# Decode attention with a long cache on one core: the second product moved to quarters of the PE array, output columns dealt, `wo` in smaller pieces

## The chip, the cores and the metric

One core of a Trainium2 chip runs the kernel. The metric is the device time in microseconds (us) of one execution, taken without a profile. All runs here are on one core; runs are called fast unless one is clearly off (one execution of 982 us among the runs of the kernel before and two of the six of e8 are such, and are left out of the ratios). TensorE is called PE below, VectorE DVE and ScalarE ACT, as in the profile. A product on PE has a stationary operand, the weights, which is loaded first (PEld in the profile), and a moving one, which is streamed through in columns; SBUF is the memory on the chip that holds the operands, PSUM the one that takes the sums. The granted clock is the share of its full clock that PE was allowed in a stretch. A landing is the moment at which a transfer's data have arrived.

## The reference

One token attends to a cache of 65,536 keys; beside it runs a small gated MLP, and a sigmoid gate mixes the two. Cut to what matters:

```python
# x (1,1,1024); 32 query heads in 4 groups of 8; K and V caches (1,4,65536,128), bfloat16
q = x @ wq                                    # 1024 x 4096
scores = q . k * 128**-0.5                    # 8 heads share one group's K and V
p = softmax(scores)                           # over 65536 keys
o = p . v                                     # the "second product"
a = o.reshape(4096) @ wo                      # 4096 x 1024
b = gated_mlp(x)  @ w_out                     # w_in 1024 x 3584, w_out 1792 x 1024
out = sigmoid(x . gate_w) * a + (1 - ...) * b # (1,1,1024), bfloat16
```

The caches are 128 MiB, all inputs 162 MB. Every byte is read once.

## The kernel before

K and V come in tiles of 128 chunks; a chunk is 128 keys, and a tile of 4 MiB is one DMA. K chunks are transposed on PE, copied to SBUF by DVE and ACT, and multiplied with the queries, which gives scores with the keys on the partitions. Five buffers (`NKV`) take all large loads in turn. The parts that the change touches:

```python
LAG = 4
WO_SPLIT = ((16,), (8, 4, 2, 1, 1))     # wo in two buffers: one piece of 16 chunks, then 8, 4, 2, 1, 1
...
    def v_units(g, j, vt):               # second product: V chunk stationary, scores moving
        ...
            for i in range(TG):          # one product for each chunk of 128 keys
                ...
                nc.tensor.matmul(o_ps[g][:, o0:o0 + wv], lhsT=vt[:, c, :],
                                 rhs=scT[g][:, lo:hi, :].rearrange("p c h -> p (c h)"),
                                 start=False, stop=(cg == NCG - 1), skip_group_check=True)
...
    def project(w, n, vec, c0, first=False, last=False):   # used for w_out and for wo
        for c in range(n):
            for j in range(NJ):                             # NJ = 8
                nc.tensor.matmul(
                    out_ps[:, j, :], lhsT=w[:, c, j * P:(j + 1) * P],
                    rhs=vec[:, c0 + c:c0 + c + 1].to_broadcast([P, W]),
                    start=(first and c == 0 and j == 0), stop=(last and c == n - 1),
                    skip_group_check=True)
...
    out_sb = const.tile([P, NJ], FP32, name="out_sb")
    nc.vector.tensor_copy(out=out_sb[:], in_=out_ps[:, :, 0])
    outT_ps = psm.tile([NJ, P], FP32, name="outT_ps", tag="m")
    nc.tensor.transpose(outT_ps[:], out_sb[:], ident_f[:])
    outT = const.tile([NJ, P], BF16, name="outT")
    nc.vector.tensor_copy(out=outT[:], in_=outT_ps[:])
    nc.sync.dma_start(out=out.rearrange("o t (j p) -> (o t j) p", p=P), in_=outT[:])
```

In the second product every chunk of V is loaded as weights, for only 8 useful columns of scores. The weights of `project` are 128 neighbouring columns.

## Time and profile before

| | before |
|---|---|
| time, median of 4 runs (of 3 when predicted: 393.51) | 393.16 us |
| span of the profiled execution | 390.8 us |
| PE busy | 78% |
| DMA share from 20 to 375 us | 1.00 to 1.01, about 429 GB/s |

These lines are from the page of the kernel before: busy time by engine, three lines of the 40 slices (each digit a tenth of the slice), and two DMA queues with packets, MB and their share of the time of 16 engines.

```profile
PE 306.5 (78%) x7080; PEld 296.8 (76%) x7080; DVE 152.3 (39%) x296; ACT 122.3 (31%) x139; POOL 1.0 (0%) x9
...
PE   0774379998888879778888888697979697996946
...
DMA  8999999999999999999999999999999999999972
GB/s 329 426 444 429 441 426 430 434 429 428 429 428 426 431 423 431 429 434 429 424 426 436 424 429 431 423 434 423 428 427 434 436 434 429 434 421 428 433 330 114
...
q1 hardware_dynamic: 6208, 162.01, 96.8%
q8 instruction: 55, 0.90, 0.8%
```

The DMA line is the one to read: nine tenths or more in every slice between the first and the last two. From the sixth slice on PE has mostly digits of 6 to 9 and waits for data. The second to last slice shows something else: 330 GB/s. Three windows of the same trace, with the stretch, its length, busy time of each engine, granted clock, DMA share and GB/s:

```profile
370.00:375.00 5.00, 2.06 (x67) 1.94 (x63) 0.00 (x0) 0.00 (x0) 0.00 (x0) 0.90 1.00 424
375.00:378.00 3.00, 0.25 (x5) 0.26 (x6) 0.00 (x0) 0.00 (x0) 0.00 (x0) 0.50 0.83 341
378.00:387.00 9.00, 8.60 (x237) 8.50 (x235) 0.00 (x0) 0.00 (x0) 0.00 (x0) 0.84 0.49 198
```

From 378 to 387 us half of the DMA engines have run out of work. The trace also holds every increment that an engine makes to a transfer's semaphore when its part has landed, sixteen for each large transfer. For the last piece of `wo` they fall into two groups of eight:

```
kernel before, last piece of wo, us of each engine's landing
377.14 377.19 377.48 377.52 377.88 378.10 378.30 379.78
385.90 386.22 387.18 387.25 387.29 387.30 387.34 387.43
```

The kernel ends soon after the slower eight. The timeline of its end, with start, duration, engine and line, operation, and in brackets what ended the idle time before it:

```profile
368.31 3.63 PEld L402 LDWEIGHTS <-wout_t 128*128 128x128 bf16 x112
368.42 3.64 PE L402 MATMUL out_ps<-uT,wout_t 128*128 128x64 bf16 x112
...
377.75 7.13 PE L402 MATMUL out_ps<-oa,wo_t 128*128 128x64 bf16 x182 [5.69 <-DMA wo_t<-in_A_wo_dram]
385.29 2.61 PE L402 MATMUL out_ps<-oa,wo_t 128*128 128x64 bf16 x74 [0.41 <-issue]
387.93 0.17 DVE L433 COPY out_sb<-out_ps 128x8 f32<-128x8 f32 x1 [18.79 <-PE out_ps L402]
388.15 0.08 PEld L435 LDWEIGHTS outT_ps<-ident_f,out_sb 128*8 128x8 f32 x1 [0.38 <-DVE out_sb L433]
388.15 0.27 PE L435 MATMUL outT_ps<-ident_f,out_sb 128*8 128x128 f32 x1 [0.26 <-DVE out_sb L433]
388.46 0.28 DVE L437 CAST outT<-outT_ps 8x128 bf16<-8x128 f32 x1 [0.37 <-PE outT_ps L435]
388.77 0.36 SPq L438 DMA_DIRECT2D out_dram<-outT  x1
```

The projection of w_out takes 3.6 us for 112 products, which start 31 ns apart, at a granted clock of 1.00. The first 58 products of `wo` start 53 ns apart, for the granted clock is 0.50 there; the others again 31 ns. PE is done 0.5 us after the last piece has landed (387.43). Then 0.84 us of copy, transpose and copy, and 2.0 us from the issue of the result's DMA to the end.

### The profile page before, as it was taken

The page shows a single profiled execution, that of the slowest core. Times are in us where ns is not written, and L with a number is a line of the kernel's source. Part 1 is how long each engine was busy: PE and PEld are TensorE (multiplying, and loading weights), DVE is VectorE, ACT ScalarE, POOL GpSimd, SP SyncE. Part 2 cuts the span into 40 slices and gives each one's busy share as a digit, 9 for nine tenths or more (in the row PEclk, how much of TensorE's full clock was granted, in tenths as well). Part 3 has the DMA queues.
Part 4 walks back from the last instruction along what each step waited for, and adds up shares of the span by engine and source line. Part 5 has one row for each costly group of instructions (what it writes and reads, how often), then busy time and mean ns, then how long its engine had stood idle before and what let it go on. Part 6 is the DMA issues. An engine that isn't in the chain of part 4 may idle for free.

```text
span 390.8 us, 14957 instructions
## 1 busy us (share of the span) xinstructions
PE 306.5 (78%) x7080; PEld 296.8 (76%) x7080; DVE 152.3 (39%) x296; ACT 122.3 (31%) x139; POOL 1.0 (0%) x9
## 2 busy tenths in 40 slices
PE   0774379998888879778888888697979697996946
PEld 0764379887888779778888878696979697896846
DVE  2011036665684335336534543275434345300100
ACT  1010025554574323324543333244524242300000
POOL 1000000000000000000000000000000000000000
PEclk9999999999999989999999999899989899899869
DMA  8999999999999999999999999999999999999972
GB/s 329 426 444 429 441 426 430 434 429 428 429 428 426 431 423 431 429 434 429 424 426 436 424 429 431 423 434 423 428 427 434 436 434 429 434 421 428 433 330 114
DMA packets 6305, 162.96 MB, mean 417 GB/s; under 512 B 740, under 2 KB 740, under 8 KB 1124
## 3 DMA queue, kind: packets, MB, share of 16 engines
q1 hardware_dynamic: 6208, 162.01, 96.8%
q8 instruction: 55, 0.90, 0.8%
q14 instruction: 6, 0.05, 0.0%
q10 hardware_dynamic: 36, 0.00, 0.0%
HBM read 162.01 MB, written 0.00 MB: 415 GB/s over the span
## 4 chain that ended last, share of the span: by engine, by line
PE 55%; DMA 32%; issue 7%; ACT 3%; DVE 1%; SPq 0%; ACTq 0%
PE tps L322 27%; DMA kn<-in_A_k_cache_dram 24%; PE spt L301 13%; PE o_ps L355 11%; DMA wo_t<-in_A_wo_dram 9%; PE out_ps L402 2%; PE o_ps L344 1%; ACT ktt L325 1%; ACT scT L288 1%; ACT scT L307 1%; SPq L84 0%; PE nb_ps L279 0%; DVE mxr L264 0%; DVE mxr L309 0%; PE mxT L271 0%
## 5 line engine op out<-in xcount | busy, mean ns | idle before, releaser
L322 PE MATMUL tps<-ident_b,kn 128*128 128x128 bf16 x2048 | 164.0, 224 | 25.6 <-DMA kn<-in_A_k_cache_dram 12.8
L327 DVE COPY ktt<-tps 128x1024 bf16<-128x1024 bf16 x171 | 116.6, 689 | 123.4 <-PE tps L322 122.9
L322 PEld LDWEIGHTS <-kn 128*128 128x128 bf16 x2048 | 124.0, 100 | 28.8 <-issue 15.3
L325 ACT COPY ktt<-tps 128x1024 bf16<-128x1024 bf16 x85 | 85.9, 1012 | 156.0 <-PE tps L322 156.0
L355 PE MATMUL o_ps<-scT,vt 128*128 128x64 bf16 (+1 forms) x2048 | 104.4, 200 | 14.4 <-issue 11.5
L301 PE MATMUL spt<-qT,ktt 128*128 128x64 bf16 (+7 forms) x2048 | 102.9, 193 | 8.9 <-issue 7.0
L355 PEld LDWEIGHTS <-vt 128*128 128x128 bf16 x2048 | 88.5, 101 | 17.0 <-issue 12.9
L301 PEld LDWEIGHTS <-ktt 128*128 128x128 bf16 x2048 | 85.6, 99 | 10.6 <-issue 8.2
L307 ACT CAST scT<-spt 128x512 bf16<-128x512 f32 x32 | 18.9, 589 | 24.8 <-PE spt L301 15.9
L344 PE MATMUL o_ps<-scT,ones_b 128*128 128x256 bf16 x64 | 18.1, 283 | 2.1 <-issue 1.4
L288 ACT ACTIVATE scT<-scT 128x1024 bf16<-128x1024 bf16 x16 | 16.4, 1056 | 6.2 <-DVE scT L284 6.2
L309 DVE TENSOR_TENSOR mxr<-scT,mxr 128x512 bf16<-128x512 bf16 x24 | 10.2, 425 | 15.8 <-ACT scT L307 14.3
L185 PE MATMUL z_ps<-xT,win_t 128*128 128x18 bf16 x224 | 13.7, 210 | 1.3 <-DMA win_t<-in_B_w_in_dram 0.8
L185 PEld LDWEIGHTS <-win_t 128*128 128x128 bf16 x224 | 13.7, 158 | 1.3 <-DMA win_t<-in_B_w_in_dram 0.9
L402 PE MATMUL out_ps<-oa,wo_t 128*128 128x64 bf16 x256 | 9.7, 204 | 6.1 <-DMA wo_t<-in_A_wo_dram 5.7
L402 PEld LDWEIGHTS <-wo_t 128*128 128x128 bf16 x256 | 9.4, 105 | 6.4 <-DMA wo_t<-in_A_wo_dram 5.8
L237 PE MATMUL q_ps<-xT,wq_t 128*128 128x1 bf16 x256 | 7.1, 165 | 7.5 <-DMA wq_t<-in_A_wq_dram 7.5
L361 DVE TENSOR_TENSOR lm<-sel_q,o_ps 128x32 f32<-128x32 f32 x4 | 0.7, 182 | 31.3 <-PE o_ps L355 31.3
L237 PEld LDWEIGHTS <-wq_t 128*128 128x128 bf16 x256 | 7.0, 104 | 7.6 <-DMA wq_t<-in_A_wq_dram 7.6
L284 DVE TENSOR_TENSOR scT<-scT,negm 128x1024 bf16<-128x1024 bf16 x16 | 10.7, 685 | 0.1
L344 PEld LDWEIGHTS <-ones_b 128*128 128x128 bf16 x64 | 6.4, 100 | 2.3 <-issue 1.6
L433 DVE COPY out_sb<-out_ps 128x8 f32<-128x8 f32 x1 | 0.2, 166 | 18.8 <-PE out_ps L402 18.8
(86 smaller groups left out, 41.6 us busy)
## 6 DMA issues: line engine op xcount, KB each, us to landing
kn<-in_A_k_cache_dram SPq DMA_DIRECT2D x16, 4096.0 KB, 29.6
vt<-in_A_v_cache_dram SPq DMA_DIRECT2D x16, 4096.0 KB, 29.5
wq_t<-in_A_wq_dram SPq DMA_DIRECT2D x2, 4096.0 KB, 29.8
win_t<-in_B_w_in_dram SPq DMA_DIRECT2D x2, 3584.0 KB, 15.2
wo_t<-in_A_wo_dram SPq DMA_DIRECT2D x1, 4096.0 KB, 34.0
wout_t<-in_B_w_out_dram SPq DMA_DIRECT2D x1, 3584.0 KB
wo_t<-in_A_wo_dram SPq DMA_DIRECT2D x1, 2048.0 KB
wo_t<-in_A_wo_dram SPq DMA_DIRECT2D x1, 1024.0 KB
```

The source lines that it names most:

```text
L185: nc.tensor.matmul(z_ps[:, hf * FC + f, :], lhsT=w[:, hf, f, :], rhs=xT[:, i * KH + c:i * KH + c + 1].to_broadcast([P, zw]), start=(i == 0 ...
L237: nc.tensor.matmul(q_ps[:, h:h + 1], lhsT=w[:, c % KH, h * DH:(h + 1) * DH], rhs=xT[:, c:c + 1], start=(c == 0 and h == 0), stop=(c == KC ...
L284: nc.vector.tensor_tensor(out=blk, in0=blk, in1=negm[:].unsqueeze(1).to_broadcast([P, CT, REP]), op=ALU.add)
L288: nc.scalar.activation(out=blk, in_=blk, func=ACT.Exp, scale=SCALE)
L301: nc.tensor.matmul(spt[g][:, o:o + n], lhsT=ktt[:, j * P:(j + 1) * P], rhs=qT[:, g * REP:g * REP + n], start=True, stop=True, skip_group_c ...
L307: nc.scalar.copy(out=blk, in_=spt[g][:].rearrange("p (c h) -> p c h", h=REP))
L322: nc.tensor.transpose(tps[:, i * P:(i + 1) * P], kn[:, u * TG + i, :], ident_b[:])
L325: nc.scalar.copy(out=ktt[:], in_=tps[:])
L327: nc.vector.tensor_copy(out=ktt[:], in_=tps[:])
L344: nc.tensor.matmul(o_ps[g][:, 2 * WL:], lhsT=ones_b[:], rhs=scT[g][:, j * CT + c:j * CT + c + SW // REP, :].rearrange("p c h -> p (c h)"), ...
L355: nc.tensor.matmul(o_ps[g][:, o0:o0 + wv], lhsT=vt[:, c, :], rhs=scT[g][:, lo:hi, :].rearrange("p c h -> p (c h)"), start=False, stop=(cg ...
L402: nc.tensor.matmul(out_ps[:, j, :], lhsT=w[:, c, j * P:(j + 1) * P], rhs=vec[:, c0 + c:c0 + c + 1].to_broadcast([P, W]), start=(first and ...
```

## The change

The intent: load far fewer weights. Now four chunks of exponentiated scores (4 x 8 = 32 columns) are stationary on one quarter of the array, and four chunks of V (512 columns) move. Four such products on the four quarters cover 16 chunks: 512 products in place of 2048. The wanted sums lie on a diagonal of the result and are picked out at the end of each group. The output columns are dealt, column p*8+j to partition p, so that the result leaves without a transpose, and `wo` comes in smaller pieces. Cut to its core:

```diff
-LAG = 4
+LAG = 3
-WO_SPLIT = ((16,), (8, 4, 2, 1, 1))
+WO_SPLIT = ((8, 8), (6, 4, 3, 2, 1))
+VC = 4
+Q = 32
...
-    pst = ctx.enter_context(tc.tile_pool(name="pst", bufs=4, space=bass.MemoryType.PSUM))
+    pst = ctx.enter_context(tc.tile_pool(name="pst", bufs=3, space=bass.MemoryType.PSUM))
...
-                nc.tensor.matmul(o_ps[g][:, o0:o0 + wv], lhsT=vt[:, c, :],
-                                 rhs=scT[g][:, lo:hi, :].rearrange("p c h -> p (c h)"),
+                for t in range(P // Q):
+                    lo = c - VC * (P // Q - t)
+                    cg = j * CT + lo
+                    nc.tensor.matmul(
+                        o_ps[g][t * Q:(t + 1) * Q, :],
+                        lhsT=scT[g][:, cg:cg + VC, :].rearrange("p c h -> p (c h)"),
+                        rhs=vt[:, lo:lo + VC, :].rearrange("p c d -> p (c d)"),
+                        start=(cg < VC * P // Q), stop=(cg + VC * P // Q >= NCG),
+                        skip_group_check=True)
... (a copy, four fp32 products and seven vector steps at the end of each group; the sums of the scores likewise)
     def project(w, n, vec, c0, first=False, last=False):
+        w = w.rearrange("p c (m j) -> p c j m", j=NJ)
...
-                    out_ps[:, j, :], lhsT=w[:, c, j * P:(j + 1) * P],
+                    out_ps[:, j, :], lhsT=w[:, c, j, :],
...
-    out_sb = const.tile([P, NJ], FP32, name="out_sb")
+    out_sb = const.tile([P, NJ], BF16, name="out_sb")
     nc.vector.tensor_copy(out=out_sb[:], in_=out_ps[:, :, 0])
-    outT_ps = psm.tile([NJ, P], FP32, name="outT_ps", tag="m")
-    nc.tensor.transpose(outT_ps[:], out_sb[:], ident_f[:])
-    outT = const.tile([NJ, P], BF16, name="outT")
-    nc.vector.tensor_copy(out=outT[:], in_=outT_ps[:])
-    nc.sync.dma_start(out=out.rearrange("o t (j p) -> (o t j) p", p=P), in_=outT[:])
+    nc.sync.dma_start(out=out.rearrange("o t (p j) -> (o t p) j", j=NJ), in_=out_sb[:])
```

`w[:, c, j, :]` takes every eighth column, so the weights of all 368 projection products (112 of w_out, 256 of `wo`) are now read with a stride.

More of the change, by code (lines that the diff above doesn't have):

```diff
@@ L19 @@
 CPS = 64
-LAG = 4
+LAG = 3
 EVAC_PAT = "vav"
-WO_SPLIT = ((16,), (8, 4, 2, 1, 1))
-SW = 256
+WO_SPLIT = ((8, 8), (6, 4, 3, 2, 1))
+VC = 4
+Q = 32
 W = 64
-WL = 96
 @with_exitstack
@@ L61 @@
     SCALE = float(DH) ** -0.5
-    assert DH == P and D % P == 0 and FH % P == 0 and P % H == 0
+    assert G * Q == P and REP * VC == Q and Q == REP * QD and DH == P and D % P == 0 and FH % P == 0 and P % H == 0
     assert S % (P * CT) == 0 and CT % CPS == 0 and CPS % TG == 0 and sum(map(sum, WO_SPLIT)) == OC
@@ L69 @@
     scp = ctx.enter_context(tc.tile_pool(name="scp", bufs=2))
-    pst = ctx.enter_context(tc.tile_pool(name="pst", bufs=4, space=bass.MemoryType.PSUM))
+    pst = ctx.enter_context(tc.tile_pool(name="pst", bufs=3, space=bass.MemoryType.PSUM))
     pss = ctx.enter_context(tc.tile_pool(name="pss", bufs=2, space=bass.MemoryType.PSUM))
     psm = ctx.enter_context(tc.tile_pool(name="psm", bufs=1, space=bass.MemoryType.PSUM))
+    psl = ctx.enter_context(tc.tile_pool(name="psl", bufs=1, space=bass.MemoryType.PSUM))
     pso = ctx.enter_context(tc.tile_pool(name="pso", bufs=1, space=bass.MemoryType.PSUM))
@@ L116 @@
     nc.gpsimd.memset(ones_f[:], 1.0)
-    pbits = const.tile([P, 3], I32, name="pbits")
+    pbits = const.tile([P, 5], I32, name="pbits")
     nc.vector.tensor_scalar(out=pbits[:, 0:1], in0=pidx[:], scalar1=P // KC - 1, scalar2=None,
                             op0=ALU.bitwise_and)
-    nc.vector.tensor_scalar(out=pbits[:, 1:2], in0=pidx[:], scalar1=OC - 1, scalar2=None,
+    nc.vector.tensor_scalar(out=pbits[:, 1:2], in0=pidx[:], scalar1=Q - 1, scalar2=None,
                             op0=ALU.bitwise_and)
-    nc.vector.tensor_scalar(out=pbits[:, 2:3], in0=pidx[:], scalar1=OC.bit_length() - 1,
+    nc.vector.tensor_scalar(out=pbits[:, 2:3], in0=pidx[:], scalar1=QD - 1, scalar2=None,
+                            op0=ALU.bitwise_and)
+    nc.vector.tensor_scalar(out=pbits[:, 4:5], in0=pidx[:], scalar1=QD.bit_length() - 1,
                             scalar2=None, op0=ALU.logical_shift_right)
-    pf = const.tile([P, 4], FP32, name="pf")
+    nc.vector.tensor_scalar(out=pbits[:, 3:4], in0=pbits[:, 4:5], scalar1=REP - 1,
+                            scalar2=None, op0=ALU.bitwise_and)
+    pf = const.tile([P, 5], FP32, name="pf")
     nc.vector.tensor_copy(out=pf[:, 0:1], in_=pidx[:])
-    nc.vector.tensor_copy(out=pf[:, 1:4], in_=pbits[:])
+    nc.vector.tensor_copy(out=pf[:, 1:5], in_=pbits[:, 0:4])
     def one_hot(shape, dtype, in0, col, name):
@@ L140 @@
     sel_i = one_hot([P, P // KC], FP32, row[:, :P // KC], 1, "sel_i")
-    sel_c = one_hot([P, OC], FP32, row[:, :OC], 2, "sel_c")
-    sel_q = one_hot([P, QD], FP32, row[:, :QD], 3, "sel_q")
+    pick = one_hot([P, Q, QD], FP32, row[:, :Q].unsqueeze(2).to_broadcast([P, Q, QD]), 2, "pick")
+    own_q = one_hot([P, QD], FP32, row[:, :QD], 3, "own_q")
+    own_h = one_hot([P, REP], FP32, row[:, :REP], 4, "own_h")
     xb_ps = psm.tile([P, 2 * P], FP32, name="xb_ps", tag="m")
@@ L244 @@
     nc.vector.tensor_copy(out=qT[:, :H], in_=q_ps[:])
-    lm = const.tile([P, H, QD], FP32, name="lm")
-    ssx = const.tile([1, H, QD], FP32, name="ssx")
+    oa = const.tile([P, OC], BF16, name="oa")
     scT, mxr, spt, o_ps, s_ps = {}, {}, {}, {}, {}
@@ L334, in v_units @@
     def v_units(g, j, vt):
-        wv = W if g + 1 < G else WL
-        wc = wv // REP
         if j == 0:
-            o_ps[g] = pso.tile([P, 2 * WL + SW], FP32, name="o_ps")
+            o_ps[g] = pso.tile([P, VC * DH], FP32, name="o_ps")
+            s_ps[g] = psl.tile([P, CPS * REP], FP32, name="s_ps")
+        gs = slice(g * Q, (g + 1) * Q)
         for u in range(CT // TG):
-            c = u * TG
-            if c * REP % SW == 0:
-                nc.tensor.matmul(
-                    o_ps[g][:, 2 * WL:], lhsT=ones_b[:],
-                    rhs=scT[g][:, j * CT + c:j * CT + c + SW // REP, :].rearrange("p c h -> p (c h)"),
-                    start=(j == 0 and c == 0), stop=(j == NT - 1 and (c * REP + SW) >= CT * REP),
-                    skip_group_check=True)
-            for i in range(TG):
-                c = u * TG + i
-                cg = j * CT + c
-                lo, hi = (cg, cg + wc) if c + wc <= CT else (cg + 1 - wc, cg + 1)
-                o0 = wv - REP - (cg - lo) * REP
-                nc.tensor.matmul(o_ps[g][:, o0:o0 + wv], lhsT=vt[:, c, :],
-                                 rhs=scT[g][:, lo:hi, :].rearrange("p c h -> p (c h)"),
-                                 start=False, stop=(cg == NCG - 1), skip_group_check=True)
@@ new lines, in v_units @@
+            c = (u + 1) * TG
+            if c % (VC * P // Q) == 0:
+                for t in range(P // Q):
[7 more added lines that the diff above has]
+                        skip_group_check=True)
@@ L358, in v_units @@
+            if c % CPS == 0:
+                cg = j * CT + c - CPS
+                nc.tensor.matmul(
+                    s_ps[g][gs, :], lhsT=ones_b[:, :Q],
+                    rhs=scT[g][:, cg:cg + CPS, :].rearrange("p c h -> p (c h)"),
+                    start=(cg == 0), stop=(cg + CPS == NCG), skip_group_check=True)
             yield
         if j == NT - 1:
-            hs = slice(g * REP, (g + 1) * REP)
-            nc.vector.tensor_tensor(out=lm[:, hs, :],
-                                    in0=sel_q[:].unsqueeze(1).to_broadcast([P, REP, QD]),
-                                    in1=o_ps[g][:, wv - REP:wv].unsqueeze(2).to_broadcast([P, REP, QD]),
-                                    op=ALU.mult)
@@ L365, in v_units @@
-            ssum = wk.tile([1, REP], FP32, name="ssum")
-            nc.vector.tensor_reduce(
-                out=ssum[:], in_=o_ps[g][0:1, 2 * WL:].rearrange("p (c h) -> p h c", h=REP),
-                axis=AX.X, op=ALU.add)
-            nc.vector.tensor_copy(out=ssx[:, hs, :],
-                                  in_=ssum[:].unsqueeze(2).to_broadcast([1, REP, QD]))
+            o_sb = wk.tile([P, VC * DH], FP32, name="o_sb")
+            nc.vector.tensor_copy(out=o_sb[:], in_=o_ps[g][:])
+            om_ps = psm.tile([P, DH], FP32, name="om_ps", tag="m")
@@ new lines, in v_units @@
+            for i in range(VC):
+                nc.tensor.matmul(
+                    om_ps[gs, :],
+                    lhsT=pick[:, i * REP:(i + 1) * REP, :].rearrange("p h q -> p (h q)"),
+                    rhs=o_sb[:, i * DH:(i + 1) * DH], start=(i == 0), stop=(i == VC - 1),
+                    skip_group_check=True)
+            ssum = wk.tile([P, REP], FP32, name="ssum")
+            nc.vector.tensor_reduce(
+                out=ssum[gs, :], in_=s_ps[g][gs, :].rearrange("p (c h) -> p h c", h=REP),
+                axis=AX.X, op=ALU.add)
@@ new lines, in v_units @@
+            nc.vector.tensor_tensor(out=ssum[gs, :], in0=ssum[gs, :], in1=own_h[gs, :],
+                                    op=ALU.mult)
+            rl = wk.tile([P, 2], FP32, name="rl")
+            nc.vector.reduce_sum(out=rl[gs, 0:1], in_=ssum[gs, :], axis=AX.X)
+            nc.vector.reciprocal(out=rl[gs, 1:2], in_=rl[gs, 0:1])
+            om = wk.tile([P, QD, OC], FP32, name="om")
+            nc.vector.tensor_tensor(
+                out=om[gs], in0=om_ps[gs, :].rearrange("p (q c) -> p q c", c=OC),
+                in1=own_q[gs, :].unsqueeze(2).to_broadcast([Q, QD, OC]), op=ALU.mult)
@@ L372, in rest @@
+            osum = wk.tile([P, OC], FP32, name="osum")
+            nc.vector.tensor_reduce(out=osum[gs, :], in_=om[gs].rearrange("p q c -> p c q"),
+                                    axis=AX.X, op=ALU.add)
+            nc.vector.tensor_scalar(out=oa[gs, :], in0=osum[gs, :], scalar1=rl[gs, 1:2],
+                                    scalar2=gate[gs, :], op0=ALU.mult, op1=ALU.mult)
     def rest(units):
@@ L382 @@
                 next(vu, None)
+                if j == 0:
+                    next(vu, None)
                 run_step()
@@ L406, in project @@
                     skip_group_check=True)
-    om_ps = psm.tile([P, OC + 1], FP32, name="om_ps", tag="m")
-    nc.tensor.matmul(om_ps[:, OC:], lhsT=ssx[:].rearrange("p h q -> p (h q)"),
-                     rhs=ones_f[0:1, 0:1], start=True, stop=True, skip_group_check=True)
-    nc.tensor.matmul(om_ps[:, :OC], lhsT=lm[:].rearrange("p h q -> p (h q)"), rhs=sel_c[:],
-                     start=False, stop=True, skip_group_check=True)
-    rl = wk.tile([P, 1], FP32, name="rl")
-    nc.vector.reciprocal(out=rl[:], in_=om_ps[:, OC:])
-    oa = const.tile([P, OC], BF16, name="oa")
-    nc.vector.tensor_scalar(out=oa[:], in0=om_ps[:, :OC], scalar1=rl[:, 0:1], scalar2=gate,
-                            op0=ALU.mult, op1=ALU.mult)
     project(load(B_w_out.rearrange("(p c) n -> p c n", c=FC), (FC, D), "wout_t"),
```

## The prediction

> **What bounds it now.** The bytes. The page shows 162.01 MB on one queue and a DMA line of 9 in nearly every slice; by windows the DMA share is 1.00 to 1.01 from 20 to 375 us at about 429 GB/s. In the trace a 32,768-byte packet takes 1.213 us on its engine, so an engine's 10.126 MB need 374.9 us; TensorE (PE) is 78% busy and waits. The DMA queue's waits for PE (257 us) are waits for a free buffer with three transfers still queued (issue to landing 29.6 us against about 9.7 us each), so they cost nothing.
>
> The last 15 us are different. The landing events come in two groups of eight engines: eight finish the last wo piece at about 377.1 to 379.8 us, eight at 385.9 to 387.4. The windows agree: DMA share about 0.5 from 378 to 387. I put the lag down to 55 instruction packets of 16 KiB (the page's instruction queue), about 7 for each late engine at an estimated 1.4 us. The Trainium skill ("Runtime: NRT & Kernel Launch", Instruction fetch mechanics) has 256 instructions in a block; PE's 14,130 rows make 55 blocks, which agrees.
>
> **What the change does.**
> - Second product: 2048 pairs of about 45 ns (32 in 1.47 us with one ones-product) become 512 matmuls of 512 columns on 32-column quarters. One alone should take about 0.22 us; if the four quarters overlap, four take little more than one (70 us less PE work), if they don't, about 110 us, no gain. Either way PE keeps up with the DMA: about zero on the time.
> - PE's program falls from 14,130 to 10,995 rows, 42 blocks instead of 55: one or two fetches less per late engine, last bytes about 1.4 us earlier (near 386.0).
> - Tail: the fp32 transpose and its second copy go (388.15 to 388.77): -0.6 us; 16-byte output rows may give 0.2 back.
> - The dealing makes the projections' weights strided by 8 elements. Contiguous, they run at 31 ns each (112 in 3.6 us). The only strided weights in the trace, the z product (stride 14), run at 60 ns with a weight load of 158 instead of 98 ns; but that was at an unknown, probably cold clock. At 60 ns the 112 + 256 matmuls take 22.1 us. They cannot start before w_out lands (368.0 now, about 366.7 after): PE ends near 389.0 instead of 387.9, and PE, not the last piece, ends the kernel. At 35 ns PE follows the last piece and ends near 386.5.
> - Fewer transposition buffers (3 for 4), longer group epilogues (a 128x512 copy, four fp32 products): some PE stalls, hidden by the queue.
>
> Span, at 60 ns: 389.0 + 0.2 + 2.0 = about 391.3 us against 390.8 (I give this 65%); at 35 ns about 388.8. On the timed scale, about 2 us higher, that is 393.9 or 391.3. Predicted: 393.2 us, 8 times in 10 between 390.5 and 395.5. Faster by over 2% 0.02, within 2% 0.95, slower 0.03.
>
> **What would show it.** Right: DMA share still 1.0 to 375 us; 42 instruction packets; the late engines' last landing 1 to 2 us earlier; PE busy time down by 50 us or more if quarters overlap; wo matmuls about 60 ns apart, back to back from w_out's landing to the end, the chain of waits ending in projection matmuls without DMA waits. Wrong: projection spaced 31 to 35 ns and waiting for each wo piece.
>
> **What would make it wrong.** Quarter matmuls that serialise and run at half clock, with drains between array modes, so that PE falls behind the DMA (slower); a lag of the late engines not due to fetches, or growing; strided loads cheap at full clock (faster by 2 us).

## The result, and the profile after

| | before | after |
|---|---|---|
| time, median of 4 runs | 393.16 us | 394.11 us (393.82 to 394.29) |
| ratio of fast runs | | 1.0023, 95% interval 1.0006 to 1.0041 |
| span of the profiled execution | 390.8 us | 392.5 us |
| copy of the result out of PSUM starts at | 387.93 us | 389.96 us |
| from there to the end of the span | 2.86 us | 2.54 us |

A ratio is the mean time of one kernel's fast runs over that of the other's of the same rounds, so not quite the ratio of the medians quoted. The two profiled executions lie 1.7 us apart, more than the runs; 2.03 us of that is PE's later end, and 0.32 us is given back by the shorter closing.

The page after, the same lines as before:

```profile
PE 299.9 (76%) x5539; PEld 255.0 (65%) x5539; DVE 160.0 (41%) x316; ACT 122.2 (31%) x139; POOL 1.0 (0%) x9
...
PE   0774379887889985979884969689949797544697
...
DMA  8999999999999999999999999999999999999971
GB/s 331 435 429 441 426 424 432 432 427 422 424 440 427 426 422 431 424 432 429 426 427 431 429 436 428 426 426 432 432 427 429 429 427 427 429 431 428 412 328 73
...
q1 hardware_dynamic: 6480, 162.01, 96.6%
q8 instruction: 43, 0.70, 0.7%
```

The DMA line is as it was; the instruction queue has 43 packets instead of 55. PE has more low digits after the middle, and its granted clock fell (0.965 before, 0.925 after). Groups of instructions of both kernels, with count, busy time, mean ns, and the idle time of the engine just before them with its main cause; first before, then after:

```profile
L322 PE MATMUL tps<-ident_b,kn 128*128 128x128 bf16 x2048 | 164.0, 224 | 25.6 <-DMA kn<-in_A_k_cache_dram 12.8
L355 PE MATMUL o_ps<-scT,vt 128*128 128x64 bf16 (+1 forms) x2048 | 104.4, 200 | 14.4 <-issue 11.5
...
L402 PE MATMUL out_ps<-oa,wo_t 128*128 128x64 bf16 x256 | 9.7, 204 | 6.1 <-DMA wo_t<-in_A_wo_dram 5.7
L402 PEld LDWEIGHTS <-wo_t 128*128 128x128 bf16 x256 | 9.4, 105 | 6.4 <-DMA wo_t<-in_A_wo_dram 5.8
```

```profile
L329 PE MATMUL tps<-ident_b,kn 128*128 128x128 bf16 x2048 | 164.7, 226 | 37.3 <-DMA kn<-in_A_k_cache_dram 35.7
...
L354 PE MATMUL o_ps<-vt,scT 128*32 128x512 bf16 x512 | 51.9, 432 | 14.9 <-DMA vt<-in_A_v_cache_dram 14.9
...
L430 PE MATMUL out_ps<-oa,wo_t 128*128 128x64 bf16 x256 | 15.7, 229 | 0.6 <-DMA wo_t<-in_A_wo_dram 0.6
L430 PEld LDWEIGHTS <-wo_t 128*128 128x128 bf16 x256 | 15.6, 171 | 0.7 <-DMA wo_t<-in_A_wo_dram 0.7
```

Two things are to be seen. The second product's records fell from 104.4 to 51.9 us (records of products on different quarters overlap, so the sum even overstates it), and the idle time before the K transposes that ends with the arrival of K grew from 12.8 to 35.7 us: the saved PE time became waiting for the DMA. And the projection's weight loads grew from 105 to 171 ns, its busy time from 9.7 to 15.7 us. The end of the timeline after:

```profile
366.88 6.92 PE L430 MATMUL out_ps<-uT,wout_t 128*128 128x64 bf16 x112 [3.18 <-DMA wout_t<-in_B_w_out_dram]
...
373.64 4.00 PE L430 MATMUL out_ps<-oa,wo_t 128*128 128x64 bf16 x64
...
378.20 11.72 PE L430 MATMUL out_ps<-oa,wo_t 128*128 128x64 bf16 x192 [0.56 <-DMA wo_t<-in_A_wo_dram]
389.96 0.17 DVE L449 CAST out_sb<-out_ps 128x8 bf16<-128x8 f32 x1 [25.12 <-PE out_ps L430]
390.16 0.35 SPq L450 DMA_DIRECT2D out_dram<-out_sb  x1
```

112 products in 6.92 us and 192 in 11.72 us, each with the last product's own 0.2 us in it, are about 60 ns each, nearly twice the 31 ns of before at full clock. From 366.88 on PE pauses only once, for 0.6 us; the last piece lands at 388.06, and PE ends 1.9 us after it. Before, it was 0.5 us. So PE ends the kernel now.

```
changed kernel, last piece of wo, us of each engine's landing
378.31 378.34 378.55 378.87 378.96 378.96 379.69 382.48
385.90 386.00 386.24 386.30 386.35 386.40 387.85 388.06
```

### The profile page after: what moved, and what is told of

It reads as the page before. It is cut to its first block, busy times and chain, and to the rows that moved or that the text cites. A ratio compares the mean times of both kernels' runs of the same rounds, so it can differ in the third digit from the quotient of the medians.

```text
span 392.5 us, 11905 instructions
## 1 busy us (share of the span) xinstructions
PE 299.9 (76%) x5539; PEld 255.0 (65%) x5539; DVE 160.0 (41%) x316; ACT 122.2 (31%) x139; POOL 1.0 (0%) x9
## 4 chain that ended last, share of the span: by engine, by line
DMA 50%; PE 42%; DVE 3%; issue 2%; ACT 1%; SPq 1%; DVEq 0%; ACTq 0%
DMA kn<-in_A_k_cache_dram 39%; PE tps L329 22%; DMA wo_t<-in_A_wo_dram 10%; PE spt L308 10%; PE o_ps L354 5%; PE out_ps L430 3%; DVE ktt L334 1%; DVE scT L291 1%; PE om_ps L372 1%; PE s_ps L362 1%; ACT scT L314 1%; ACT ktt L332 1%; SPq L85 0%; DVE o_sb L369 0%; PE nb_ps L286 0%
## 5 line engine op out<-in xcount | busy, mean ns | idle before, releaser
L329 PE MATMUL tps<-ident_b,kn 128*128 128x128 bf16 x2048 | 164.7, 226 | 37.3 <-DMA kn<-in_A_k_cache_dram 35.7
L308 PE MATMUL spt<-qT,ktt 128*128 128x64 bf16 (+7 forms) x2048 | 104.0, 194 | 6.8 <-issue 6.7
L308 PEld LDWEIGHTS <-ktt 128*128 128x128 bf16 x2048 | 87.0, 100 | 8.4 <-issue 8.1
L354 PE MATMUL o_ps<-vt,scT 128*32 128x512 bf16 x512 | 51.9, 432 | 14.9 <-DMA vt<-in_A_v_cache_dram 14.9
L354 PEld LDWEIGHTS <-scT 128*32 128x32 bf16 x512 | 15.3, 100 | 26.7 <-issue 21.0
L430 PE MATMUL out_ps<-oa,wo_t 128*128 128x64 bf16 x256 | 15.7, 229 | 0.6 <-DMA wo_t<-in_A_wo_dram 0.6
L430 PEld LDWEIGHTS <-wo_t 128*128 128x128 bf16 x256 | 15.6, 171 | 0.7 <-DMA wo_t<-in_A_wo_dram 0.7
L362 PE MATMUL s_ps<-scT,ones_b 128*32 128x512 bf16 x32 | 13.4, 418 | 0.0
L369 DVE COPY o_sb<-o_ps 128x512 f32<-128x512 f32 x4 | 2.7, 684 | 26.0 <-PE o_ps L354 26.0
L430 PE MATMUL out_ps<-uT,wout_t 128*128 128x64 bf16 x112 | 6.9, 235 | 3.2 <-DMA wout_t<-in_B_w_out_dram 3.2
```

The source lines that it names most:

```text
L308: nc.tensor.matmul(spt[g][:, o:o + n], lhsT=ktt[:, j * P:(j + 1) * P], rhs=qT[:, g * REP:g * REP + n], start=True, stop=True, skip_group_c ...
L329: nc.tensor.transpose(tps[:, i * P:(i + 1) * P], kn[:, u * TG + i, :], ident_b[:])
L354: nc.tensor.matmul(o_ps[g][t * Q:(t + 1) * Q, :], lhsT=scT[g][:, cg:cg + VC, :].rearrange("p c h -> p (c h)"), rhs=vt[:, lo:lo + VC, :].re ...
L362: nc.tensor.matmul(s_ps[g][gs, :], lhsT=ones_b[:, :Q], rhs=scT[g][:, cg:cg + CPS, :].rearrange("p c h -> p (c h)"), start=(cg == 0), stop= ...
L430: nc.tensor.matmul(out_ps[:, j, :], lhsT=w[:, c, j, :], rhs=vec[:, c0 + c:c0 + c + 1].to_broadcast([P, W]), start=(first and c == 0 and j ...
```

## The experiments

Theory A: the strided weights make the projection twice as slow, so that PE, no longer the last landing, ends the kernel. Rival B: the loss lies elsewhere in the change, in landings that the quarters, the pieces or the clock delay. Theory F: eight of the sixteen DMA engines are late because they carry PE's instruction packets, about an eighth of them each. Rival G: the lag belongs to those engines or to the data. Theory H: the quarters did buy PE time, which lies idle because the DMA is the limit.

Each experiment was timed in five rounds against the kernel before on the same chip. e1 to e4, e5 to e8, e9 and e10, e11 and e12 shared a chip; all results were correct.

| run | median us | ratio to before | last landing | PE done (copy starts) |
|---|---|---|---|---|
| before | 393.16 | | 387.43 | 387.93 |
| after | 394.11 | 1.0023 | 388.06 | 389.96 |
| e1 contiguous weights | 393.02 | 1.0001 (0.9989 to 1.0013) | 388.03 | 388.53 |
| e2 e1, results by 2-byte elements | 405.60 | 1.0315 | 387.78 | 388.28 |
| e3 before with dealing | 397.74 | 1.0119 | 387.62 | 393.55 |
| e4 e1 with 2048 more PE instructions | 402.92 | 1.0248 | 396.87 | 397.38 |
| e5 the same, elsewhere | 400.40 | 1.0194 | 388.18 | 396.27 |
| e6 e1, one piece on few DMA engines | 402.45 | 1.0247 | 397.87 | 398.80 |
| e7 e3 with the new pieces of wo | 395.04 | 1.0070 (1.0044 to 1.0095) | 387.56 | 390.80 |
| e8 before with 2048 more PE instructions | 420.91 (419.69 of the 4 fast runs) | 1.0662 | 413.92 | 416.05 |
| e9 after, finer pieces | 393.59 | 1.0019 (1.0006 to 1.0032) | 388.06 | 389.14 |
| e10 e9, 600 PE instructions fewer | 392.61 | 0.9992 (0.9978 to 1.0006) | 387.00 | 388.08 |
| e11 e10, still finer | 392.95 | 0.9999 (0.9986 to 1.0011) | 387.28 | 388.05 |
| e12 after again | 393.99 | 1.0023 (1.0009 to 1.0037) | 387.91 | 389.80 |

### e1: the changed kernel with contiguous weights

```diff
-        w = w.rearrange("p c (m j) -> p c j m", j=NJ)
-                    out_ps[:, j, :], lhsT=w[:, c, j, :],
+                    out_ps[:, j, :], lhsT=w[:, c, j * P:(j + 1) * P],
... (and the transpose and second copy at the end put back)
```

> The changed kernel with the projections' weights contiguous again and the fp32 transpose at the end put back; everything else of the change kept. Theory A (the strided weights make PE end the kernel): projection matmuls 31 ns apart instead of 60, PE waits for the late pieces of wo and ends about 0.5 us after the last one lands (388.5 in a span like that of the changed kernel, against 389.96), the closing steps cost 0.3 us more: about 1.1 us faster than the changed kernel, level with or a little under the kernel before. Rival B (the loss lies elsewhere in the change, for instance in DMA landings that the quarters, the clock or the pieces of wo delay): no gain, or under 0.4 us.

Measured: 1.0001 of the kernel before, 1.1 us under the changed kernel's median. The end of its timeline:

```profile
386.18 0.92 PE L429 MATMUL out_ps<-oa,wo_t 128*128 128x64 bf16 x24 [0.22 <-DMA wo_t<-in_A_wo_dram]
...
387.44 1.06 PE L429 MATMUL out_ps<-oa,wo_t 128*128 128x64 bf16 x24 [0.34 <-DMA wo_t<-in_A_wo_dram]
388.53 0.17 DVE L448 COPY out_sb<-out_ps 128x8 f32<-128x8 f32 x1 [23.42 <-PE out_ps L429]
```

PE waits for the late pieces again and ends 0.5 us after the last landing, with landings as in the changed kernel (388.03 and 388.06). That is theory A in place and number; rival B falls. (Its products start 31 ns apart at a granted clock of 1.00, and 53 ns at 0.50, which the granted clock was for part of this stretch.) It also says what all the rest of the change is worth in time: nothing that five rounds can see.

### e2: contiguous weights without a transpose

```diff
-    nc.sync.dma_start(out=out.rearrange("o t (p j) -> (o t p) j", j=NJ), in_=out_sb[:])
+    nc.sync.dma_start(out=out.rearrange("o t (j p) -> (o t p) j", p=P), in_=out_sb[:])
```

> As e1, but without the transpose: the 1024 results leave from 128 partitions as 2-byte elements to column j*128+p. Theory A: PE ends as in e1; the closing steps save 0.6 us of PE and vector work, and the 1024 small elements (64 for each engine, some 10 ns each by the 9 ns packets of the trace) cost 0.5 to 1 us: within 0.5 us of e1. If the small writes are dear, 2 us slower than e1.

Measured: 12.6 us more than e1. PE was done at 388.28, again 0.5 us after the last landing, so that contiguous weights alone, without the transpose of e1, bring PE's end back. The DMA was issued at 388.48; its last part landed at 401.51. The 1024 elements of 2 bytes are far dearer than the 9 ns of their packet records, on which I had built the expectation. The Trainium skill ("DMA: Bandwidth & Descriptors", Specifications) puts the least size for full rate at 512 B and says that smaller ones are read, modified and written; this run agrees that small writes are dear, and shows that 13 us can go into 2 KB. The changed kernel's rows of 16 bytes took 2.3 us from issue to end, against 2.0 us for the rows of 256 bytes before. So the dealing was a sound way to drop the transpose, for its own closing; its price lies in the weights.

### e3: the dealing alone, in the kernel before

```diff
+        w = w.rearrange("p c (m j) -> p c j m", j=NJ)
-                    out_ps[:, j, :], lhsT=w[:, c, j * P:(j + 1) * P],
+                    out_ps[:, j, :], lhsT=w[:, c, j, :],
... (and the closing of the changed kernel, without a transpose)
```

> The kernel before with the dealing alone: strided weights, results out as 16-byte rows without a transpose. Theory A: the projections run at 60 ns from about 368.3, 368 of them take 22.1 us, PE ends near 390.6 instead of 387.9, closing steps 0.3 us shorter: 2 to 2.5 us slower than the kernel before. Rival B: the dealing is harmless or helps by the 0.3 to 0.6 us of the removed transpose.

Measured: 4.7 us slower, twice what I expected. I had let PE run from w_out to the end without a pause, but with the pieces of before it can't:

```profile
368.67 6.89 PE L403 MATMUL out_ps<-uT,wout_t 128*128 128x64 bf16 x112
...
377.94 15.57 PE L403 MATMUL out_ps<-oa,wo_t 128*128 128x64 bf16 x256 [2.39 <-DMA wo_t<-in_A_wo_dram]
393.55 0.17 DVE L434 CAST out_sb<-out_ps 128x8 bf16<-128x8 f32 x1 [24.17 <-PE out_ps L403]
```

It waits until 377.94 for the piece of 16 chunks, and then has all 256 products of 61 ns before it. So the size of the pieces decides how much of the slower projection shows.

### e7: the dealing and the new pieces, in the kernel before

```diff
-WO_SPLIT = ((16,), (8, 4, 2, 1, 1))
+WO_SPLIT = ((8, 8), (6, 4, 3, 2, 1))
... (on e3)
```

> e3 (kernel before, strided weights, no transpose) with the changed kernel's pieces of wo, (8, 8), (6, 4, 3, 2, 1), and nothing else of the change. If the first piece of 16 chunks was what made e3 cost 4.7 us (PE sat idle until 377.9 and then had 256 products of 60 ns to do), PE now starts on the first eight chunks right after w_out and ends near 390.7: 2 to 2.8 us under e3, 2 to 2.5 us over the kernel before. If the dealing costs more than PE time, it stays within 1 us of e3.

Measured: 1.0070, 2.7 us under e3's median and some 2.3 us over the kernel before, as expected (one of its six runs was slower, 398.3). PE runs from 368.5 to 390.8 without a wait:

```profile
368.51 6.90 PE L403 MATMUL out_ps<-uT,wout_t 128*128 128x64 bf16 x112
...
375.24 15.52 PE L403 MATMUL out_ps<-oa,wo_t 128*128 128x64 bf16 x256
...
390.80 0.17 DVE L434 CAST out_sb<-out_ps 128x8 bf16<-128x8 f32 x1 [21.58 <-PE out_ps L403]
```

The changed kernel starts that chain 1.6 us earlier, at 366.88. Some 1.2 us of this is w_out's landing (366.83 against 368.01 in e7; the two differ by 12 instruction packets, to which e5 and e10 come back), and 0.5 us is the second product of the last tile, which in e7 is done at 367.1 and with its closing steps lets w_out's products start at 368.5; with the quarters it is done by 362. Here, through an earlier end of the second product and perhaps through fewer instruction packets, the quarters shorten the path: the changed kernel's ratio is 1.0023 against 1.0070 in e7.

### e9: finer pieces for the changed kernel

```diff
-WO_SPLIT = ((8, 8), (6, 4, 3, 2, 1))
+WO_SPLIT = ((4, 4, 4, 4), (4, 4, 3, 2, 2, 1))
... (and w_out in two halves, each projected when it has landed)
```

> The changed kernel, weights still strided, no transpose, but w_out loaded in two halves and wo in pieces of 4, 4, 4, 4, 4, 4, 3, 2, 2, 1 chunks. Theory A says PE loses because it waits for a whole eight-chunk piece (until 378.2 in the changed kernel) and then has 192 products of 60 ns left; a chunk takes PE 0.48 us and the DMA 0.61 us, so with small pieces PE keeps up: it ends 0.5 us after the last landing (388.6 instead of 389.96), about 1.3 us faster than the changed kernel, 0.3 to 0.6 us under the kernel before. If the strided weights cost more than that chain shows, or the smaller pieces slow the DMA, it stays at the changed kernel's time.

Measured: 1.0019; 0.5 us under the changed kernel's median and not the 1.3 us expected. By the ratios, each to the kernel before on its own chip, it comes to 0.2 us (1.0019 and 1.0023, with intervals that overlap), so it is not clear that there is a gain. PE now starts w_out at 364.31 and pauses for each of four pieces, but then:

```profile
380.61 2.14 PE L430 MATMUL out_ps<-oa,wo_t 128*128 128x64 bf16 x32 [0.30 <-DMA wo_t<-in_A_wo_dram]
...
383.08 6.03 PE L430 MATMUL out_ps<-oa,wo_t 128*128 128x64 bf16 x96 [0.34 <-DMA wo_t<-in_A_wo_dram]
389.14 0.17 DVE L453 CAST out_sb<-out_ps 128x8 bf16<-128x8 f32 x1 [23.67 <-PE out_ps L430]
```

A chunk costs PE about 0.50 us (6.03 us for 12 chunks) and the DMA 0.63 us (5.03 us for the last 8, from 383.03 to 388.06). PE gains only 0.13 us on each chunk, so the 2 us with which it starts on a piece of four are not made good in eight chunks; it ended 1.1 us after the last landing. Theory A's place is right; my claim that such pieces let PE keep up was wrong.

### e4 and e8: the same extra work for the changed and for the old second product

```diff
-        for j in range(TG):
+        for j in (*range(4), *range(TG)):       # half the score products twice, same operands
... (e4 on e1, e8 on the kernel before)
```

> e1 with half of the score products issued twice (the same operands, overwritten by the same values), 2048 more PE instructions in the middle of the kernel, no other change. Theory F (eight DMA engines are late by the instruction packets they carry): 8 instruction packets more (about 51), the eight early engines unchanged, the late ones 1.4 to 1.6 us later, and the time 1 to 1.6 us above e1. Rival G (the lag is a property of these engines or of the data): the landings and the time stay as in e1, for PE has the time.

> The kernel before with half of its score products doubled, as e4 did to e1. Theory H (the quarters bought PE time that lies idle because the DMA is the limit): with the same load added, the kernel before, which has about 60 us more of PE work, starves the DMA longer than e4: 404 us or more, the share of the DMA under 1.00 in stretches beyond 150 us too. Rival: as e4 within 2 us (402.9), that is, the quarters gave PE no usable headroom.

e4 did not test what it was made for: PE got so much to do that it freed K and V buffers too late, and the DMA starved (a share of 0.72 from 120 to 150 us). The DMA slices of e4, then those of e8:

```profile
DMA  8999999999997949999999999999999999999993
```

```profile
DMA  8999999999998499999999988999799969899993
```

e4 has one hole, at 120 to 150 us, and costs 9.9 us over e1; e8 has holes up to 365 us, and its four fast runs cost 26 us over its own kernel before. With the same load added to both, the kernel with the quarters is some 16 us faster, each held against the kernel before on its own chip. (e1 also has other pieces of `wo`, a shorter LAG and one transposition buffer less, which no run separates from the quarters here.) So theory H holds: the gain of the quarters is real, and is PE headroom that this kernel does not need. That the four quarters overlap is seen in the trace: groups of four products start within 10 to 20 ns, and the groups follow 215 ns apart at full clock (338.932, 339.147, 339.362 us), for four times 512 columns. The Trainium skill ("TensorE: Matmul & The Clock Gate", Part 3) describes such overlap for tiles of the array, about 4 ns apart; this trace agrees.

### e5: more instructions where PE has slack

```diff
-        for j in range(TG):
+        for j in (*range(4 if g >= 2 else 0), *range(TG)):
... (and after each unit of the last group's second product:)
+                for i in range(8):
+                    nc.tensor.matmul(pad_ps[:, i:i + 1], lhsT=ones_b[:], rhs=ones_b[:, 0:1],
+                                     start=True, stop=True, skip_group_check=True)
```

> e4 starved the DMA at 120 to 150 us and so tested nothing about the late engines. Here e1 gets 2048 more PE instructions only where PE has slack: half the score products doubled in head groups 2 and 3, and 8 one-column products to a scratch bank after each unit of the last group's second product. Theory F (late engines carry the instruction packets): 51 packets instead of 43, the median of the eight early engines' last landing unchanged (378 to 379), the median of the eight late ones 1.3 to 1.7 us later than e1's 386.3, no slice of the DMA under 9 before the tail, and the time 0.5 to 1.7 us above e1. Rival G (the lag belongs to the engines or the data): late landings within 0.4 us of e1's and the time as e1.

The time missed: the added products made PE late in the last group, and it ended at 396.27. The landings, which PE did not delay (no slice of the DMA line below is under 9 before the last two), give the answer. Times are us; early and late are the medians of the eight earlier and the eight later landings of the last piece.

| run | instruction packets | early | late | lag | lag for each eighth of the packets |
|---|---|---|---|---|---|
| before | 55 | 377.70 | 387.27 | 9.57 | 1.39 |
| e3 | 55 | 378.59 | 387.51 | 8.91 | 1.30 |
| e7 | 55 | 378.74 | 387.37 | 8.63 | 1.26 |
| after | 43 | 378.91 | 386.33 | 7.41 | 1.38 |
| e1 | 43 | 378.82 | 386.30 | 7.48 | 1.39 |
| e5 | 51 | 378.63 | 387.80 | 9.16 | 1.44 |
| e10 | 41 | 379.24 | 386.64 | 7.40 | 1.44 |

Eight packets more than e1 moved the late engines by 1.50 us and the early ones by -0.18 us. Theory F holds for the change of the lag, and G, which had no change, falls. How much one packet costs its engine is less sure than the first rows suggest: over the runs whose DMA did not starve (e2, e9, e11 and e12 give 1.36 to 1.41) it is 1.26 to 1.44 us if the whole lag is put down to packets, and e3 and e7, with 55 packets like the kernel before, have the lowest figures. That a fixed part of the lag belongs to the engines is not ruled out. The packets' own records last 0.95 us on average before and 1.06 us after; where the rest comes from is open.

```profile
DMA  8999999999999999999999999999999999999940
...
q1 hardware_dynamic: 6352, 162.01, 95.0%
q8 instruction: 51, 0.84, 0.9%
```

### e10: fewer instructions

```diff
-    z_part(0)
-    z_part(1)
+    zrow = as_rows(win_t, F, "zrow")
+    qrow = as_rows(wq_t, HD, "qrow")
... (on e9; 480 products with the weights of w_in and wq stationary become 120 products with x
     stationary, 32 equal columns on each quarter, and 60 one-column products that sum and turn)
```

> e9 with 600 PE instructions fewer: the z and q products as rows (x stationary on quarters, weights moving in 512 columns, summed and turned by one-column products with 1/32). Theory F read backwards: 40 or 41 instruction packets instead of 43, so no late engine carries a sixth before the end: the two latest landings (387.8 and 388.0) come down to the others' 386.3, the time 1 to 1.7 us under e9 and 1.3 to 2.3 us under the kernel before. Rival G: landings as in e9. If the row products hold up the first K tiles, the DMA share falls under 0.95 in some slice before 200 us and the time rises.

Measured: 41 packets, the last landing at 387.00 instead of 388.06, and 1.0 us less than e9, beside it on the same chip. The two latest engines are no longer later than the rest, as F says of a sixth packet that is gone; the other six stayed where they were. The 1.3 to 2.3 us under the kernel before that I expected did not come: the ratio is 0.9992, with an interval that includes 1.

```profile
q1 hardware_dynamic: 7056, 162.01, 97.1%
q8 instruction: 41, 0.67, 0.7%
```

### e11 and e12: still finer pieces, and the changed kernel again

```diff
-WO_SPLIT = ((4, 4, 4, 4), (4, 4, 3, 2, 2, 1))
+WO_SPLIT = ((4, 4, 4, 4), (4, 3, 3, 2, 1, 1, 1, 1))
... (e11, on e10)
```

> e10 with the last pieces of wo as 4, 3, 3, 2, 1, 1, 1, 1 chunks. In e10 PE ended 1.1 us after the last landing, for it gains only some 0.13 us a chunk on the DMA and still carried part of a four-chunk piece. If that is the reason, PE now ends 0.5 us after the last landing and the time falls by 0.4 to 0.6 us, to about 0.997 of the kernel before; if small pieces cost the DMA more than they save, no gain.

> The changed kernel as it is, timed again with five rounds on the chip of e11, to hold its ratio against the experiments: 1.002 to 1.004 of the kernel before if its loss of about 1 us is real; within 0.001 of 1 if it was a matter of the chip.

In e11 PE ended 0.8 us after the last landing instead of 1.1, but the landings came 0.3 us later and the closing took 3.1 instead of 2.7 us: 0.9999, no gain, where 0.997 was expected. No version here is clearly faster than the kernel before. e12 repeats the changed kernel's ratio, 1.0023, so its loss of about 1 us is not a matter of one chip.

### e6: one piece of wo on the low-numbered DMA engines

```diff
-            nc.sync.dma_start(out=t[:, c0 - b:c0 - b + n, :], in_=wo_view[:, c0:c0 + n, :])
+            for p0, p1 in ((0, 119), (119, P)) if n == 4 else ((0, P),):
+                nc.sync.dma_start(out=t[p0:p1, c0 - b:c0 - b + n, :],
+                                  in_=wo_view[p0:p1, c0:c0 + n, :])
... (on e1)
```

> e1 with the four-chunk piece of wo loaded as 119 partitions and 9 partitions. By the Trainium skill (DMA: Bandwidth & Descriptors, how many engines) 119 rows go to the 7 lowest-numbered engines, 17 each. If the late engines are not among them, the early seven take over some 3 us of work and the late ones are rid of 2.4 us: last landing near 385.6 instead of 388.0 and the time 2 to 2.5 us below e1, so below both kernels. If the late engines are the low ones, the last landing moves to about 391 and the time is 3 us above e1. If they are mixed, in between and above e1. If the split is not as stated, as e1.

Measured: 9 us slower, worse than any of the cases laid out. The split was as the skill states it: the transfer of 119 rows made 7 increments when data landed, that of 9 rows 9. Of the 7 landings, four came at 382.0 to 384.5 and three at 387.2 to 393.8, so early and late engines seem to be mixed among the low-numbered. But pieces issued before it also landed later than in e1 (the second piece of eight chunks at 381.35 instead of 377.90), which the order of issue does not explain. Moving work to the early engines in this way failed; why it slowed the others is open.

## Why the prediction was right, and where it was not

The measured 394.11 us lies in the range given, the class (within 2%) was right, and so was the branch held more likely. The range of 5 us held both branches (391.3 and 393.9), so it is the trace, not the time, that tells them apart.

- "The bytes" bound the kernel: right. The DMA share stayed at 1.00 from 20 to 375 us after the change.
- Quarters that overlap, about zero on the time: right on both counts (215 ns for a group of four; e1, with all of the change but the dealing, is level with before). "PE busy time down by 50 us or more" was wrong as a test: the page's PE line went from 306.5 to 299.9 us only. A record is longer at a lower clock (the 512-column product with ones took 0.38 us at a granted clock near 1.00 and 0.63 us at 0.50), and the line counts more than array time (records of 0.38 us, where groups of four follow 215 ns apart). The idle time waiting for K shows the gain better, and e4 against e8 best.
- The strided weights at 60 ns: right, measured 60.0 ns in every stretch of the projection, at full and at half clock alike. That was the open question of the prediction, which guessed that z had run at a cold, that is lower, clock. The windows that I had asked of the trace answer it: from 10 to 50 us, where z ran, the granted clock of the kernel before was 1.00. What depends on the clock is the contiguous product: 31 ns at 1.00 and 53 ns at 0.50 (`wo` before, w_out and `wo` in e1). So the dealing nearly doubles the time at full clock and costs about 7 ns a product at half clock. The Trainium skill ("TensorE: Matmul & The Clock Gate", Weight-path perf modes) lists fast weight loads for packed or strided reads alike; these runs show that a stride of 8 elements costs about 30 ns a product at full clock.
- "PE ends near 389.0": measured 389.96. The term that was mis-sized is the chain from w_out to the end, taken as 22.1 us without a pause. It had one: the next product could have started at 377.48 (373.64 and 64 times 60 ns) and started at 378.20, when the second piece of eight chunks had landed, whose last engine was 1.7 us behind the others. The other 0.2 us is the last product's own length (229 ns is the group's mean), which the count left out.
- "Last bytes about 1.4 us earlier (near 386.0)": wrong in size, and nearly in sign; they landed at 388.06, against 387.43. Right was the cause of the change in the lag (e5, e10) and the count, 43 packets for 42 predicted (the trace has 11,078 PE rows, 43.3 times 256, where the prediction counted 10,995). The step that failed is the taking of "one or two fetches less per late engine" for a gain of all: six late engines did come near 386.3, but two, which by theory F still carried one packet more, landed near 388, and a transfer is done when its last engine is. The early engines were also 1.2 us later than before. e3, with the same loads and pieces as the kernel before, had its early engines at 378.59, so about 0.9 us of that is seen between two runs of the same transfers; the cause is open. The error hid, because PE and not the last landing ended the kernel.
- The closing: 0.6 us were expected from the dropped transpose, less 0.2 for the small rows; measured 0.32.

Added up, the profiled spans differ by 1.7 us where 0.5 was predicted for this branch; the timed medians differ by 0.95 us. That the branch's own 393.9 us lies only 0.2 us from the measurement is luck: its span was 1.2 us too short (391.3, measured 392.5), and to get from the span to the timed scale it added 2.6 us, where its text says about 2 and the profiled execution of the changed kernel has 1.8 (394.29 and 392.5). The point prediction, 393.2, is a mixture of the two branches and was 0.9 us low.

## What to carry to other kernels

When the DMA is busy from end to end, PE time saved in the middle turns into waiting; look for the end of the last bytes and what follows it. There, a change of layout that saves a microsecond of closing steps can cost more if it makes the weight loads strided, and how much of that shows depends on how finely the last loads are cut: with PE only a fifth faster than the DMA, it can't make up for one large piece. Also count instructions: in this program of 11,000 to 14,000 PE rows their fetches delayed eight of the DMA engines, and the last piece waits for the latest of these.

## What the Trainium skill lacked or had wrong

- "TensorE: Matmul & The Clock Gate", Weight-path perf modes: packed and strided weight reads are listed as alike. A bfloat16 128x128 load with a stride of 8 elements spaced products 60 ns apart at full and at half clock (w_in's stride of 14 gave 60 ns too, at full clock); contiguous ones ran at 31 ns with 64 moving columns (53 ns at half clock), and at 27 ns with one. No page has a time for a strided weight load; the general remark on strided reads under "SBUF — State Buffer" has none either.
- "Runtime: NRT & Kernel Launch", Instruction fetch mechanics: the cost of a block of instructions is called mostly hidden. With the DMA saturated, eight blocks of 16 KiB more put eight of the DMA engines 1.5 us later (e5 against e1), and with 55 blocks they were 8.6 to 9.6 us behind the other eight. The size of the block agrees: 55, 43 and 41 packets for the 14,160, 11,078 and 10,478 PE rows of the traces of before, after and e10, which are 55.3, 43.3 and 40.9 times 256.
- No page says that the packets fall on eight of the sixteen engines. That is inferred here from the two groups of eight landings and from e5; the packets' records don't name an engine.
- "DMA: Bandwidth & Descriptors": it warns of small transfers and of layouts that make a descriptor of each element, but has no time for writes of single elements. 1024 writes of 2 bytes took 13.0 us from issue to landing; 128 rows of 16 bytes cost 0.3 us more than 8 rows of 256.
- The same page, how many engines: its count of 7 engines for 119 rows agrees with e6. It doesn't warn that pieces issued before such a transfer can land later (3.5 us for the second piece of eight chunks in e6); why they did is open.
